# Linear attention and a GELU MLP on one core: k and v nine tokens to a partition, kv in two row tiles, first MLP blocks by token quarters, another load order, stores from ScalarE's queue

## Chip, cores, metric

One Trainium2 chip, one core. The metric is the device time of one launch in microseconds, as the median of several runs. For one core a run's state is taken from its time alone; every run below counts as fast. Each set of runs below was made on one chip with the kernel before beside it, so kernels are compared by their ratio to before. The granted clock is the TensorE clock that the profile shows for a stretch, 1.00 being full speed. PSUM is the memory that matmuls write to, in banks. In the diffs below, comments behind `#` are mine.

## The reference

```python
phi = lambda x: np.where(x > 0, x, np.exp(x) - 1.0) + 1.0        # q, k, v: (8, 8, 576, 64) float32
kv  = einsum('bhsd,bhse->bhde', phi(k), v);  z = phi(k).sum(axis=2)
att = einsum('bhsd,bhde->bhse', phi(q), kv) / (einsum('bhsd,bhd->bhs', phi(q), z)[..., None] + 1e-6)
x   = att.transpose(0, 2, 1, 3).reshape(4608, 512)
out = gelu_tanh(x @ w_in) @ w_out                                # w_in (512, 2048), w_out (2048, 512)
```

## The kernel before

A sequence has 576 tokens: 512 of them ("main") lie four to a partition, and the 64 left over ("rest") of two sequences share one tile. The MLP runs in nine blocks of 512 tokens (eight batches, then all rests together): 16 h steps (w_in, then gelu on ScalarE), then 16 o steps (w_out). Work of other batches is put behind a numbered step of a block (`at(block, step, fn)`), so program order on each engine is set by hand. Cut to what the argument touches:

```python
for c in range(C):                                   # kv of one head pair: 4 matmuls of all 128 rows ...
    nc.tensor.matmul(dst, lhsT=kp[:, c, P*i:P*(i+1)], rhs=vps[b%2][:, 2*i:2*i+2, c, :], start=(c==0), stop=False)
nc.tensor.matmul(dst, lhsT=kr[r, 0, P*i:P*(i+1)], rhs=vrs[..][b%2][r, 2*i:2*i+2, :], start=False, stop=True)  # ... and the rest

for c in range(C + 1):                               # prologue: numerator of batch 0
    if c < C:
        nab_mm(qt[:, c], kvbds[0], n_ps); x_c.append(nab_evac(n_ps))
        keep_warm(2)                                 # matmuls of zeros
    if c >= 1:
        t_x(x_c[c-1], tv); nc.scalar.copy(xt[:, :, P*(c-1):P*c], tv[:, 0:NP, :])
# ... then gelu table, block 0

load_slots = {2: (0, 8), 3: (0, 27), 4: (1, 22)}     # batch 4 is loaded behind step 22 of block 1
# batch 1: exps at (0,15), kv at (0,19), numerator at (0,23..26)
# batch 3: prepare at (1,15): exps 15, phi k 17, cast v 19, phi q 22; numerator of batch 2 at (1,15),(1,17),(1,19),(1,21)
# x and q of batches 2.. are transposed by DMA from SyncE's queue; stores and loads use the same queue
```

## Time and profile before

| | before |
|---|---|
| time, median | 322.5 us |
| span in the profile | 320.0 us |
| third h step of block 0 ends | 26.6 us |
| first o step of block 0 | 37.8 us |
| third h step of block 1 ends | 66.7 us |
| first h step of block 2 | 102.9 us |

The marks cut the span at places that both kernels have. A mark is read from the timeline: the start of the row of h or o matmuls, plus 0.863 us for each step of four matmuls, or 0.83 us for the last 12 short ones where tokens come in quarters.

### The profile page before, as it was taken

The numbers are of one execution on the slowest core, as the hardware profiler recorded it, in microseconds if no ns is written. First come the engines' busy times: TensorE is split into PE (matmuls) and PEld (weight loads), VectorE is DVE, ScalarE is ACT, GpSimd is POOL, SyncE is SP. The second block draws the span as 40 slices with busy tenths as digits, with TensorE's granted clock in tenths as the row PEclk, the third lists the DMA queues.
The fourth block names the chain that finished last, engine by engine and source line by source line (L and its number), as shares of the span: only waits on it lengthen the run. The fifth ranks groups of instructions, "written<-read, shape, count | busy, mean of one in ns | idle before, by whom it ended". The sixth has DMA issues, their size and how long they took to land.

```text
span 320.0 us, 4083 instructions
## 1 busy us (share of the span) xinstructions
PE 294.1 (92%) x1586; PEld 141.6 (44%) x1586; DVE 128.1 (40%) x239; ACT 160.7 (50%) x215; POOL 9.4 (3%) x22
## 2 busy tenths in 40 slices
PE   8969929969969976999999999999999999999993
PEld 3534415524524532445445544544454444444441
DVE  3763077666394223853191439335533000000011
ACT  4737792096723553725744583568355036216500
POOL 6040000000000000000000000000000000000000
PEclk9999978998979997999999999999999999999998
DMA  7999989952115996966599458630245110011022
GB/s 260 340 405 380 387 264 361 359 200 66 34 40 78 283 323 117 338 159 144 117 355 186 132 151 294 198 64 3 66 147 69 66 68 0 0 66 68 0 66 67
DMA packets 75332, 53.74 MB, mean 168 GB/s; under 512 B 44081, under 2 KB 68657, under 8 KB 75313
## 3 DMA queue, kind: packets, MB, share of 16 engines
q1 hardware_dynamic: 75312, 53.49, 56.5%
q8 instruction: 12, 0.20, 0.3%
q14 instruction: 8, 0.06, 0.1%
HBM read 36.70 MB, written 9.44 MB: 144 GB/s over the span
## 4 chain that ended last, share of the span: by engine, by line
PE 68%; DVE 2%; DMA 1%; ACT 1%; issue 0%; DVEq 0%
PE o_ps L557 33%; PE h_ps L538 30%; PE n_ps L236 2%; PE kv_ps L200 1%; DMA xt<-x 1%; DVE k_p L157 1%; ACT k_e L148 1%; DVE x L248 0%; PE kv_ps L208 0%; DVE k_e L153 0%; DVE o_sb L572 0%; DVE o_sb L569 0%; ACT o_sb L570 0%; DVE r L246 0%; DVEq L569 0%
## 5 line engine op out<-in xcount | busy, mean ns | idle before, releaser
L557 PE MATMUL o_ps<-w_out_sb,g 128*128 128x512 bf16 x576 | 130.4, 384 | 0.0
L538 PE MATMUL h_ps<-xt,w_in_sb 128*128 128x512 bf16 x512 | 122.1, 385 | 3.6 <-ACT g L545 2.9
L545 ACT ACTIVATE g<-h_ps 128x512 bf16<-128x512 f32 x144 | 85.4, 597 | 55.9 <-PE h_ps L538 55.8
L557 PEld LDWEIGHTS <-g 128*128 128x128 bf16 x576 | 56.5, 99 | 66.9 <-issue 3.8
L538 PEld LDWEIGHTS <-w_in_sb 128*128 128x128 bf16 x576 | 54.7, 98 | 62.5 <-issue 7.0
L574 ACT COPY o_sb<-o_ps 128x512 f32<-128x512 f32 x17 | 10.0, 585 | 81.0 <-PE o_ps L557 45.6
L572 DVE COPY o_sb<-o_ps 128x512 f32<-128x512 f32 x18 | 12.4, 686 | 64.6 <-PE o_ps L557 64.6
L248 DVE TENSOR_TENSOR x<-n_ps,r 128x512 bf16<-128x512 f32 x36 | 24.9, 691 | 6.5 <-DMA xt<-x 5.3
L225 DVE CAST kvbd<-kv_ps 64x260 bf16<-64x260 f32 x15 | 6.4, 427 | 36.4 <-PE kv_ps L208 36.3
L246 DVE RECIPROCAL r<-n_ps 128x8 f32<-128x8 f32 x36 | 7.4, 206 | 33.7 <-PE n_ps L236 33.7
L153 DVE TENSOR_SCALAR k_e<-k_e 128x2048 bf16<-128x2048 bf16 (+1 forms) x9 | 5.7, 637 | 37.1 <-ACT k_e L148 32.7
L157 DVE SCALAR_TENSOR_TENSOR k_p<-k_x,k_e 128x512 bf16<-128x512 f32 (+1 forms) x36 | 20.3, 626 | 0.3
L157 DVE SCALAR_TENSOR_TENSOR q_p<-q_x,q_e 128x512 bf16<-128x512 f32 (+1 forms) x36 | 20.3, 626 | 0.3
L200 PE MATMUL kv_ps<-vp,k_p 128*128 128x130 bf16 x128 | 13.4, 231 | 6.0 <-DVE vp L185 6.0
L236 PE MATMUL n_ps<-kvbd,qt 128*128 128x130 bf16 x128 | 13.0, 224 | 4.8 <-DVE x L248 4.3
L288 PE MATMUL w_ps<-warm 128*128 128x512 bf16 x50 | 14.8, 445 | 1.2 <-DVE warm L120 1.2
L200 PEld LDWEIGHTS <-k_p 128*128 128x128 bf16 x128 | 10.3, 102 | 12.5 <-issue 4.0
L236 PEld LDWEIGHTS <-qt 128*128 128x128 bf16 x128 | 9.6, 99 | 12.9 <-issue 4.0
L538 PE MATMUL h_ps<-xt_rest,w_in_sb 128*128 128x512 bf16 x64 | 14.0, 379 | 0.0
L148 ACT ACTIVATE k_e<-k_x 128x2048 bf16<-128x2048 f32 x7 | 13.4, 1911 | 0.1
L148 ACT ACTIVATE q_e<-q_x 128x2048 bf16<-128x2048 f32 x7 | 13.3, 1897 | 0.0
L185 DVE CAST vp<-v_x 128x2048 bf16<-128x2048 f32 x7 | 8.5, 1220 | 0.0
(52 smaller groups left out, 105.1 us busy)
## 6 DMA issues: line engine op xcount, KB each, us to landing
out_dram<-o_sb SPq DMA_DIRECT2D x16, 512.0 KB, 3.1
k_x<-in_k_dram SPq DMA_DIRECT2D x7, 1024.0 KB, 6.9
q_x<-in_q_dram SPq DMA_DIRECT2D x7, 1024.0 KB, 9.0
v_x<-in_v_dram SPq DMA_DIRECT2D x7, 1024.0 KB, 9.4
w_st<-in_moe_w_in_dram SPq DMA_DIRECT2D x4, 1024.0 KB, 10.1
w_st<-in_moe_w_out_dram SPq DMA_DIRECT2D x4, 1024.0 KB, 10.7
k_x<-in_k_dram SPq DMA_DIRECT2D x2, 512.0 KB, 4.2
q_x<-in_q_dram SPq DMA_DIRECT2D x2, 512.0 KB, 6.5
```

The costliest lines, as they stand in the source:

```text
L148: nc.scalar.activation(e, ld[name, b], AF.Exp)
L157: nc.vector.scalar_tensor_tensor(xp[:, c, hs, :], xv[:, c, hs, :], 0.0, ev[:, c, hs, :], op0=ALU.max, op1=ALU.add,)
L185: fn(out=vps[b % 2][:, s, :, 0:D], in_=ld["v", b][:, s].rearrange("p h (c d) -> p h c d", d=D),)
L200: nc.tensor.matmul(dst, lhsT=kp[:, c, P * i : P * (i + 1)], rhs=vps[b % 2][:, 2 * i : 2 * i + 2, c, :], start=(c == 0), stop=False,)
L236: nc.tensor.matmul(n_ps[rows, i // 2, 2 * E * (i % 2) : 2 * E * (i % 2) + 2 * E], lhsT=qt_c[:, i, rows], rhs=kvbd[:, i, :], skip_group_che ...
L248: nc.vector.tensor_tensor(x, n_v[:, :, :, 0:D], r[:, :, :, None].to_broadcast([P, 2, 4, D]), op=ALU.mult,)
L288: nc.tensor.matmul(w_ps, lhsT=warm[:, 0:P], rhs=warm)
L538: nc.tensor.matmul(h_ps, lhsT=w_in_sb[:, c, P * m : P * (m + 1)], rhs=xt[:, c, :], start=(c == 0), stop=(c == KM - 1),)
L545: nc.scalar.activation(g[:, m, :], h_ps, AF.Gelu_apprx_tanh)
L557: nc.tensor.matmul(o_ps, lhsT=g[:, m, P * t : P * (t + 1)], rhs=w_out_sb[:, m, :], start=(m == 0), stop=(m == MM - 1),)
L572: nc.vector.tensor_copy(dst, o_ps)
L574: nc.scalar.copy(dst, o_ps)
```

## The change

Its intent: no small loads and no rest matmuls for k and v; the prologue's MLP starts as soon as 128 tokens are ready; weights come before batch 1, whose attention then no longer stands in TensorE's way with its data missing; SyncE no longer holds stores. The diff, cut to its core (`...` marks cuts):

```diff
-    def load_main(src, b, name, eng, parts=1): ...   # 4 tokens a partition, 1024-byte runs
-    def load_rest_half(src, t, m, s, eng): ...       # 64 tokens, 256-byte runs
+    def pairs(src, b):                               # two heads fill 128 partitions, 9 tokens each, 2304-byte runs
+        return src[b].rearrange("h s d -> (h s d)").rearrange("(u n f) -> n u f", n=P, f=J * D)
...
+    def kv_mm(b, ii, kv_ps, js=range(J)):
+        for j in js:                                 # 9 tokens
+            for a in range(2):                       # even heads in rows 0-63, odd heads in rows 64-127
+                r = slice(HP * a, HP * (a + 1))
+                nc.tensor.matmul(kv_ps[:, a, 2*E*ii:2*E*(ii+1)], lhsT=kp[r, j, 2*ii:2*ii+2, :],
+                                 rhs=vp[r, j, 2*ii:2*ii+2, :], start=(j == 0), stop=(j == J - 1), ...)
...
+        nab0(0); nab0(1)                             # prologue: no keep_warm in this loop any more
+        for c in range(C):
+            xs[c] = nab_evac(n_pss[c]); t_x(xs[c], t_ps)
+            if c + 2 < C: nab0(c + 2)
+            nc.scalar.copy(xt[:, :, P*c:P*(c+1)], t_ps)
+            for m in range(QUARTERS):                # QUARTERS = 3: h steps 0..2 on these 128 tokens
+                h_mm(h_pss[m], xt, m, slice(P*c, P*(c+1)))
... # batch 1: cast v, transpose q at (0,30), kv and the same chunk loop at (0,31)
+        at(j, 30, lambda: cast_v(b, slice(0, 1), nc.scalar.copy))
+        at(j, 30, lambda: cast_v(b, slice(1, NP), nc.vector.tensor_copy))
... # block 1: h 0-7, o fourths 0-1, h 8-15, o fourths 2-3
+    plan_prepare(2, 1, 7, (0, 1, 3, 5))
+    plan_attention(2, 1, (16, 17, 18, 19), 19, (21, 23, 25, 27))   # kv in four pieces
+    plan_prepare(3, 1, 23, (0, 1, 4, 5))             # phi of k of batch 3 at step 24
+    at(*((1, 28) if b == 4 else (b - 3, 15)), lambda b=b: load_batch(b))
-            nc.sync.dma_start(out=ov[:, t - 1 : t + 1, :], in_=o_sb)
+            nc.scalar.dma_start(out=ov[:, t - 1 : t + 1, :], in_=o_sb)
```

## The prediction

> **What bounds the kernel now.** I read the page first (busy shares), then the table of stretches, then the timeline around each place where TensorE's clock or busy share drops, and last the chain that ended last.
>
> ```profile
> PE 294.1 (92%) x1586; PEld 141.6 (44%) x1586; DVE 128.1 (40%) x239; ACT 160.7 (50%) x215; POOL 9.4 (3%) x22
> 24.02 13.97 PE L538 MATMUL h_ps<-xt,w_in_sb 128*128 128x512 bf16 x64 [0.67 <-ACT xt L345]
> 186.20 13.81 PE o_ps L557 x64
> 171.54 0.23 PE kv_ps L200 x4
> ```
>
> TensorE is the bound. In the chain a run of 64 MLP matmuls takes 13.81 us, 215.8 ns each, and there are 18 such runs (9 token blocks, two layers): 18 x 13.81 = 248.6 us that the change leaves alone. The other 71 us of the 320.0 us span are: the prologue until the first MLP matmul (24.0), the tail after the last (4.8), attention matmuls between the MLP ones, and waits. From 140 to 260 us there are no waits at all: one block takes 29.7 us there (140.10 to 169.82), 27.6 of MLP plus 1.16 for kv (four groups of five matmuls, 0.29 each) plus 0.93 for the numerator (4 x 0.23). So the waits sit in the first 128 us:
>
> ```profile
> 47.46 0.59 PE L200 MATMUL kv_ps<-vp,k_p 128*128 128x130 bf16 x4 [6.02 <-DVE vp L185]
> 71.48 5.30 PE L538 MATMUL h_ps<-xt,w_in_sb 128*128 128x512 bf16 x16 [2.91 <-ACT g L545]
> 92.68 0.59 PE L236 MATMUL n_ps<-kvbd,qt 128*128 128x130 bf16 x4 [2.82 <-DVE x L248]
> 122.81 0.66 PE L236 MATMUL n_ps<-kvbd,qtr 128*64 128x130 bf16 x8 [4.69 <-DVE x L248]
> ```
>
> The bracket is TensorE's idle time before the row and what ended it: 6.02 + 2.91 + 2.82 + 4.69 = 16.4 us. Each costs more than itself. The table of stretches (us from:to, length, busy time of PE, PEld, DVE, ACT, POOL with counts, granted clock, DMA share, GB/s) shows the clock behind each:
>
> ```profile
> 47.46:51.50 4.04, 4.04 (x26) 2.86 (x26) 3.96 (x8) 2.36 (x2) 0.00 (x0) 0.55 1.08 381
> 71.50:75.10 3.60, 3.60 (x9) 1.29 (x9) 3.50 (x7) 2.49 (x6) 0.00 (x0) 0.53 0.02 5
> 92.70:95.60 2.90, 2.90 (x11) 1.28 (x12) 2.83 (x5) 0.00 (x0) 0.00 (x0) 0.52 0.22 45
> 122.80:127.00 4.20, 4.19 (x25) 1.76 (x26) 0.90 (x2) 1.66 (x2) 0.00 (x0) 0.59 0.60 64
> ```
>
> Lost: 4.04 x 0.45 + 3.60 x 0.47 + 2.90 x 0.48 + 4.20 x 0.41 = 6.6 us more. The waits are worth about 23 us, and that is what a change of order can win.
>
> **What the Trainium skill says.** "TensorE: Matmul & The Clock Gate", Part 1, says that the array falls to half clock after an idle window of about 3.4 us and needs about as long to recover. The trace agrees on the recovery (0.52 to 0.59 for 2.9 to 4.2 us), but idle times of 2.8 and 2.9 us were already enough here. "TensorEngine Tiling (Array Packing)", Key Properties, says that different tiles work in parallel but that changing the tiling mode drains the array. The trace has both:
>
> ```profile
> 15.00 0.23 PE L208 MATMUL kv_ps<-vr,kr_p 64*128 64x130 bf16 x1
> 15.16 0.41 PE L200 MATMUL kv_ps<-vp,k_p 128*128 128x130 bf16 x4
> 184.79 0.44 PE L236 MATMUL n_ps<-kvbd,qtr 128*64 128x130 bf16 x8
> 185.16 1.04 PE L538 MATMUL h_ps<-xt,w_in_sb 128*128 128x512 bf16 x4
> ```
>
> In the prologue one 64-row matmul stands between groups of four full ones, and the period is 0.50 us (15.00 to 15.50) where the all-128-row groups later take 0.29: 0.21 us for a switch there and back. The eight half-column matmuls at 184.79 take 0.37 us with the switches in it, where 8 x 0.058 = 0.46 would be serial: the halves overlap in part. "DMA: Bandwidth & Descriptors", Issuing engines are not separate DMA queues, says a second issuing queue saves only the issuing sequencer's time; so moving stores to ScalarE frees SyncE's order, not bandwidth. "ScalarE activation tables: per-element evaluation and per-set limits", What a function is on this engine, gives 1283 ns for a table load; the trace has 1283.
>
> **The change part by part.**
>
> Prologue, to the end of the third h block (before: 24.02 + 3 x 0.863 = 26.6 us). Loads: the first 2.2 MB (q and k halves) had landed by 9.7 us before and will again, then v by about 12.8. ScalarE: the last exp of k 9.5 to 10.7 (1.06 x 1152/1024 = 1.17), the table load, now early, to 12.0, the qt copy (1.0) to 13.0, casts of v to 14.8. VectorE's phi of 1024 + 1152 elements twice ends near 13.2. So kv starts at 14.2 and ends at 15.4; its two evacuations end at 16.45 (before 17.16), x0 is ready at 17.85 (before 18.58). From there the old loop took 1.43 us a chunk and then began MLP. The new one does 12 matmuls of 128 columns per chunk as soon as the chunk is copied: transposes 0.4, copy 0.65, 12 x 0.058 = 0.7, in order on TensorE, 1.76 us a chunk. First quarter at 19.0, the last ends at 19.0 + 3 x 1.76 + 0.7 = 25.0. **Gain 1.6.**
>
> From there to the third h block of block 1 (before 66.7, so 40.1 us). Thirteen h blocks end at 36.2. k of batch 1 (after 10.75 MB, at 360 to 390 GB/s about 34.5 us) and q (37) now arrive before ScalarE is free. ScalarE: table, exps (2 x 1.17, 2 x 1.06), table, until 44.0. VectorE: two phi_k of 2.0 and phi_q of 3.45 end near 47. v lands at 43. So kv of batch 1 is put at the end of the o run (50.9), and the 6.02 us wait and its cold clock (1.8) go. But now nothing lies beside that attention: transposes 0.95, kv 1.2, qt copies and evacuations to about 53.7, x0 at 55.1, then four chunks of 1.76 with the quarters in them, ending at 62.2. 62.2 - 25.0 = 37.2. **Gain 2.9.**
>
> Block 1 to its end (before 66.7 to 103.1, 36.4 us). New order: 8 h, two fourths of o, 8 h, the rest. The exps of batch 2 lie beside o, so the 2.91 wait on gelu and its 1.7 of cold clock go. New waits: kv of batch 2 is at slot 16, nine steps (7.8 us) after the exps; ScalarE and VectorE need about 9.5 (gelu end 0.8 after, table 1.28, exp 2.15, clamp 0.77, four of 0.76, cast 1.37): 1.7 us. And the 2.82 wait comes back larger. The exps of batch 3 are at slot 23, phi_k at 24, and the evacuations of the numerator of slots 25 and 27 stand behind phi_k in VectorE's order. From the last h to x: 0.8 + 1.28 + 2.15 + 0.77 + 3.05 + 0.95 = 9.0 us; TensorE has 4 x 0.863 + 0.5 = 3.95 us of work until it needs that buffer. Wait 5.1, then 1.7 of cold clock. Sum: 25.0 of MLP + 1.8 kv + 0.9 + 1.7 + 5.1 + 1.7 = 36.2. **Gain 0.2.**
>
> Blocks 2 to 8 and the tail (before 216.9). The wait of 4.69 was a chain: x buffers stood full because their transposes queued on SyncE behind loads of 64-row rests (3.5 us of issue each) and behind stores. The rests of k and v are gone, and the stores are on ScalarE; it and its cold clock (1.7) go. kv now has 36 matmuls of 64 rows in four pieces. At the pace of the column halves (0.37/8 = 0.046 with switches) that is 1.66; at 18 pairs of 0.058 plus 4 x 0.21 it is 1.88. I take 1.8, so 0.64 more than 1.16, five times: 3.2. 193.4 MLP + 5 x 2.73 + 1.5 for the query rests + 4.8 tail = 213.4. **Gain 3.5.** VectorE and ScalarE get somewhat longer k and v pieces (2304 for 2048) but keep slack in every block.
>
> Span 25.0 + 37.2 + 36.2 + 213.4 = 311.8; the time is 2.5 us above the span (322.5 against 320.0): **314.3 us**, 2.5% less.
>
> **Rivals.** (1) *The row tiles do not overlap.* Then kv costs 36 x 0.058 + 0.84 = 2.9 us a batch, 6 us more over the remaining batches: 321, the same. For it: only the column form is in this trace; and two weight loads per pair may not fit in 0.058. Against: the overlap of the halves. (2) *The wait in block 1 is not there or hidden*, because the chain ScalarE, VectorE is shorter than I add up: 307 to 309. For it: the author tuned these slots. Against: the same chain produced the 2.82 wait, and it now has two steps less to hide in. (3) *The attention of batch 1, alone on TensorE, drops the clock* or store issue on ScalarE delays its copies (load traffic is heaviest there; one store issue took 1.92 us at its longest): 316 to 319. (4) *The front gains more*, since k and v come in runs of 2304 bytes, not 1024: prologue 1 us shorter, 313.
>
> **Range and chances.** The terms I am least sure of are kv (-1 to +6), the wait in block 1 (-6 to +2) and batch 1's attention (-1 to +4). That makes 307 to 321. The 2% line is 316.1, close to the middle: faster 0.60, within 2% 0.36, slower 0.04.
>
> **What would show it.** h block 3 starts near 25; no 6 us wait for vp near 47; iteration 1 has h rows with no wait on g at its start, but an n_ps row near 88 us waiting about 5 us for DVE x, with a clock near 0.5 behind it; no n_ps wait on xt transposes near 115; later blocks 30.3 us and kv pieces of 0.4 to 0.5 us. The prediction is wrong if that wait is missing, or if a later block takes over 31 us.

## The result, and the profile after

325.9 us against 322.5: 1.013 times before (95% interval 1.009 to 1.016). Ratios here are the mean time of one kernel's fast runs over that of the other's of the same rounds, so not quite the ratio of the medians quoted. The prediction of 314.3 us with 321 as its upper end was wrong; the change is slightly slower. Measured once more in a later set of runs (after_again), it was 1.012.

| mark (us) | before | predicted | after | after_again |
|---|---|---|---|---|
| third h step of block 0 ends | 26.6 | 25.0 | 24.5 | 27.2 |
| first o step of block 0 | 37.8 | 36.2 | 38.7 | 39.6 |
| third h step of block 1 ends | 66.7 | 62.2 | 67.0 | 66.1 |
| first h step of block 2 | 102.9 | 98.4 | 102.6 | 102.6 |
| span | 320.0 | 311.8 | 323.9 | 322.4 |

The table of marks says where to look. In the first profile the prediction loses 3.0 us between the first two marks, 2.3 in the next stretch, gains 0.6 in block 1 and loses 7.9 from block 2 on: 311.8 - 0.5 + 3.0 + 2.3 - 0.6 + 7.9 = 323.9. In the second profile of the same kernel (after_again, whose rows are read like the others) the four stretches up to block 2 lose 2.2, 1.2, 0.5 and 0.4 us instead: other places, and about the same sum. TensorE's waits of over 1.1 us behind the prologue's start of work, in the timeline of the changed kernel (first profile):

```profile
13.81 1.25 PE L225 MATMUL kv_ps<-vp,k_p 64*128 64x130 bf16 x36 [1.56 <-ACT vp L215]
25.77 0.43 PE L275 MATMUL h_ps<-xt,w_in_sb 128*128 128x512 bf16 x1 [1.22 <-ACT g L285]
80.31 0.46 PE L225 MATMUL kv_ps<-vp,k_p 64*128 64x130 bf16 x10 [1.22 <-DVE vp L215]
97.18 0.40 PE L246 MATMUL n_ps<-kvbd,qt 128*128 128x130 bf16 x4 [4.73 <-DVE x L258]
122.83 0.65 PE L246 MATMUL n_ps<-kvbd,qtr 128*64 128x130 bf16 x8 [4.36 <-DVE x L258]
```

The waits of 6.02 and 2.91 us are gone, as predicted. The one near 97 is the predicted 5.1. The one at 122.8 was to go and is there, nearly as long as before (4.36 us for 4.69). The second, 1.22 us, is new. I read it so: the first whole h step takes over PSUM banks from the prologue's three h tiles and waits until the gelus have read them (a_pool tests this). And the clock falls where no long wait stands (table of stretches, same columns as in the prediction; the changed kernel first, then the kernel before):

```profile
16.00:20.00 4.00, 2.55 (x36) 2.12 (x36) 2.65 (x7) 2.00 (x3) 1.90 (x1) 1.00 1.06 389
24.00:28.00 4.00, 2.56 (x15) 1.29 (x14) 0.00 (x0) 2.01 (x4) 2.75 (x2) 0.75 1.06 388
28.00:32.00 4.00, 4.00 (x17) 1.65 (x16) 0.00 (x0) 1.99 (x5) 2.94 (x2) 0.83 1.05 388
56.00:60.00 4.00, 2.11 (x18) 1.68 (x18) 1.74 (x5) 0.96 (x2) 0.00 (x0) 0.59 1.05 393
60.00:64.00 4.00, 3.76 (x37) 3.48 (x36) 1.12 (x3) 0.78 (x2) 0.00 (x0) 0.56 1.05 324
```

```profile
16.00:20.00 4.00, 2.66 (x21) 1.29 (x19) 2.20 (x5) 0.63 (x2) 3.20 (x2) 1.00 1.05 408
24.00:28.00 4.00, 3.98 (x19) 1.85 (x19) 1.91 (x3) 3.39 (x5) 0.00 (x0) 1.00 1.07 394
28.00:32.00 4.00, 4.00 (x20) 1.76 (x18) 0.56 (x1) 2.67 (x6) 0.00 (x0) 1.00 1.11 364
56.00:60.00 4.00, 3.84 (x33) 2.27 (x33) 3.08 (x9) 0.00 (x0) 0.00 (x0) 1.00 1.11 332
60.00:64.00 4.00, 4.00 (x26) 2.07 (x25) 2.48 (x5) 0.58 (x1) 0.00 (x0) 1.00 1.09 386
```

Before, the clock was 1.00 in all of them. In this profile the changed kernel runs at 0.75 and 0.83 where its first whole h steps stand, and at little over half clock in the first two of batch 1's four chunks (12 matmuls of 128 tokens take 1.44 us there and 0.83 in the other two).

What stands in SyncE's queue ahead of the transposes that the wait at 122.8 is for (SyncE's timeline, changed kernel; the second column is the time the issue takes):

```profile
108.31 0.58 SPq L80 DMA_DIRECT2D k_x<-in_k_dram  x1
108.95 1.09 SPq L90 DMA_DIRECT2D q_x<-in_q_dram  x2
110.15 1.08 SPq L80 DMA_DIRECT2D v_x<-in_v_dram  x1
111.74 3.25 SPq L470 DMA_TRANSPOSE qtr<-qr_p  x1
115.11 8.79 SPq L460 DMA_TRANSPOSE xt<-x  x4
```

And two lines of the same queue in the kernel before, where rests do stand in front, as the prediction read:

```profile
105.58 3.49 SPq L75 DMA_DIRECT2D v_r<-in_v_dram  x2
117.49 6.39 SPq L435 DMA_TRANSPOSE xt<-x  x4
```

Stores and k and v rests are gone from the changed kernel's queue, and yet its four transposes take 8.8 us to issue. The first three lines are the loads of batch 4: 1.18 + 1.05 + 1.18 = 3.4 MB. They are issued at 108.3, 5.5 us later than the first of batch 4's loads before (102.8).

### The profile page after: what moved, and what is told of

It reads as the page before. It is cut to its first block, busy times and chain, and to the rows that moved or that the text cites. A ratio compares the mean times of both kernels' runs of the same rounds, so it can differ in the third digit from the quotient of the medians.

```text
span 323.9 us, 4353 instructions
## 1 busy us (share of the span) xinstructions
PE 293.5 (91%) x1732; PEld 141.0 (44%) x1763; DVE 118.6 (37%) x210; ACT 165.2 (51%) x222; POOL 16.4 (5%) x20
## 4 chain that ended last, share of the span: by engine, by line
PE 80%; DVE 4%; ACT 3%; DMA 2%; issue 1%; ACTq 0%; DVEq 0%
PE h_ps L275 38%; PE o_ps L600 36%; PE kv_ps L225 3%; PE n_ps L246 2%; DMA xt<-x 2%; DVE k_p L175 2%; ACT k_e L178 1%; DVE vp L215 1%; ACT L178 1%; ACT xt L536 1%; DVE x L258 1%; PE t_ps L268 0%; DVE k_e L172 0%; DVE o_sb L559 0%; ACT g L285 0%
## 5 line engine op out<-in xcount | busy, mean ns | idle before, releaser
L600 PE MATMUL o_ps<-w_out_sb,g 128*128 128x512 bf16 x564 | 128.9, 386 | 0.9 <-issue 0.2
L275 PE MATMUL h_ps<-xt,w_in_sb 128*128 128x512 bf16 (+1 forms) x567 | 123.7, 361 | 5.9 <-ACT xt L378 2.2
L275 PEld LDWEIGHTS <-w_in_sb 128*128 128x128 bf16 x648 | 58.4, 100 | 63.9 <-issue 9.1
L172 DVE TENSOR_SCALAR k_e<-k_e 128x2304 bf16<-128x2304 bf16 (+1 forms) x10 | 6.6, 656 | 53.4 <-ACT k_e L178 53.4
L175 DVE SCALAR_TENSOR_TENSOR k_p<-k_x,k_e 128x576 bf16<-128x576 f32 x32 | 22.3, 754 | 0.3
L178 ACT ACTIVATE k_e<-k_x 128x2304 bf16<-128x2304 f32 (+1 forms) x10 | 17.3, 1738 | 1.0 <-DMA k_x<-in_k_dram 0.9
L178 ACT ACTIVATE q_e<-q_x 128x2048 bf16<-128x2048 f32 (+1 forms) x10 | 15.5, 1556 | 3.0 <-DMA q_x<-in_q_dram 3.0
L225 PE MATMUL kv_ps<-vp,k_p 64*128 64x130 bf16 x288 | 12.8, 218 | 4.0 <-DVE vp L215 2.1
L225 PEld LDWEIGHTS <-k_p 64*128 64x128 bf16 x288 | 8.3, 94 | 14.8 <-issue 10.9
L215 DVE CAST vp<-v_x 128x2304 bf16<-128x2304 f32 (+2 forms) x8 | 10.8, 1353 | 0.0
```

The costliest lines, as they stand in the source:

```text
L175: nc.vector.scalar_tensor_tensor(o, x, 0.0, e, op0=ALU.max, op1=ALU.add)
L178: nc.scalar.activation(e[:, s], ld[name, b][:, s], AF.Exp)
L215: fn(out=vps[b % 2][:, :, us, 0:D].rearrange("p j u d -> p u j d"), in_=ld["v", b][:, us].rearrange("p u (j d) -> p u j d", d=D),)
L225: nc.tensor.matmul(kv_ps[:, a, 2 * E * ii : 2 * E * (ii + 1)], lhsT=kp[r, j, 2 * ii : 2 * ii + 2, :], rhs=vp[r, j, 2 * ii : 2 * ii + 2, :] ...
L275: nc.tensor.matmul(h_ps[:, ts], lhsT=w_in_sb[:, c, P * m : P * (m + 1)], rhs=xt[:, c, ts], start=(c == 0), stop=(c == KM - 1), skip_group_ ...
L600: nc.tensor.matmul(o_pss[t], lhsT=g[:, m, P * t : P * (t + 1)], rhs=w_out_sb[:, m, :], start=(m == 0), stop=(m == MM - 1),)
```

## The experiments

Theory after the result, in four parts. **L**: the wait in block 2 comes from batch 4's loads in front of the x transposes, not from stores and rests. **C**: the two stretches with little work for TensorE lose the clock, and that ate what the prologue and batch 1 should have gained. **H**: the hand-over of PSUM banks costs 1.2 us. **K**: kv costs more in pieces because TensorE changes between whole and half rows. Rivals: the stores and rests (my prediction's step), too few x buffers, a clock that doesn't matter because TensorE waits for others anyway, row halves that don't overlap.

### Batch 4's loads earlier, in both kernels

```diff
-        at(*((1, 28) if b == 4 else (b - 3, 15)), lambda b=b: load_batch(b))      # a_load4
+        at(*((1, 13) if b == 4 else (b - 3, 15)), lambda b=b: load_batch(b))
```
```diff
-        at(*load_slots.get(b, (b - 3, 15)), lambda b=b: load_batch(b))      # b_load4; for batch 4 this was step 22 of block 1
+        if b == 4:
+            at(1, 8, lambda: load_batch(4, "kqv"))       # with the rests of k and v
+            at(1, 22, lambda: load_batch(4, "r"))        # the rest of q alone
```

> The changed kernel with one edit: the loads of batch 4 are issued at step 13 of block 1 instead of step 28. Theory L (loads in front): in block 2 of both kernels the transposes of x stand in SyncE's queue behind batch 4's loads (3.4 MB, some 9 us of traffic), so x's buffers stay full and TensorE waits 4.4 us near 122.8 us with half a clock for 5.6 us after it. Then the wait near 122.8 goes, and the time falls from 325.9 by about 6.5 us to 319 to 320. Rival S, the step of my prediction: the wait comes of stores and small rest loads in SyncE's order; both are already gone in the changed kernel, so moving these loads would change nothing (within 1 us). Rival X: three x buffers are too few whatever the queue does; the wait then stays too.

> The kernel before, with batch 4's loads (k, q, v and the rests of k and v) issued at step 8 of block 1 instead of step 22; the rest of q stays at 22, for its buffer comes free late. Theory L: TensorE's wait of 4.69 us near 122.8 and its cold clock go here too: 322.5 falls to about 316.5. Rival S (stores and the small rests are what holds the transposes up): the rest loads of q and the stores still stand in front, so 1 to 3 us at most.

Measured: a_load4 321.2 us, 0.997 of before (0.992 to 1.003), so 1.5% below the changed kernel's 1.012; b_load4 316.4 us, 0.982 (0.976 to 0.988). In block 2 the matmuls for the query rest follow without a bracket in both. In a_load4:

```profile
105.35 1.89 PE L275 MATMUL h_ps<-xt,w_in_sb 128*128 128x512 bf16 x8 [1.45 <-DMA xt<-x]
121.20 0.43 PE L246 MATMUL n_ps<-kvbd,qtr 128*64 128x130 bf16 x8
```

The wait is gone in both kernels, so L holds, and the wait was there without the change. A caution: b_load4 moves the rests of k and v along with the loads, so what these rests cost in the kernel before is not separated; a_load4 has no such rests, so there it is the loads alone. The query rest's transpose takes 3.25 us to issue behind the loads (above) and 1.19 us in a_load4. In a_load4 the loads now stand in front of batch 2's transposes and cost 1.45 us there: its gain is 5 us and not the 6.5 expected. X falls, and for the changed kernel S falls.

### Stores from ScalarE's queue alone

```diff
-            nc.sync.dma_start(out=ov[:, t - 1 : t + 1, :], in_=o_sb)      # the kernel before, both stores
+            nc.scalar.dma_start(out=ov[:, t - 1 : t + 1, :], in_=o_sb)
```

> The kernel before with one edit: its stores are issued from ScalarE's queue. The step of my prediction: stores in SyncE's order are part of what held the transposes of x up in block 2; then the wait of 4.69 us near 122.8 shrinks by 1 to 3 us and the time by 1 to 4. Theory L (batch 4's loads in front): the wait stays at 4 us or more and the time within 1 us of before.

Measured: 322.2 us, 1.000 of before (0.995 to 1.006). The wait is even longer in its profile:

```profile
122.20 0.66 PE L236 MATMUL n_ps<-kvbd,qtr 128*64 128x130 bf16 x8 [5.45 <-DVE x L248]
```

Moving the stores is worth nothing in time, which is the second half of why my step failed.

### PSUM pools, then matmuls of zeros

a_pool opens the main pools (six banks "ho", one pair "a") at the start and uses them in the prologue. a_poolwarm adds zeros:

```diff
-        keep_warm(2)                      # before kv of batch 0
+        keep_warm(7)                      # also 2 more before the numerator, 4 after it, 2 in each chunk
...
+            kv_evac(b, kv_ps, ...); warm1(5)          # batch 1; 5 after the numerator, 2 in each chunk
```

> The changed kernel with the PSUM pools of the main part used from the start, in place of three prologue pools that are given back (numerator single-buffered in the prologue, as in batch 1). Theory H (hand-over): the h block after the first three waits 1.2 us for the three gelus because its banks are taken over from the prologue's; that wait goes and the time falls by about 1 us. The clock of the prologue is not helped by it: a stretch of 3 to 8 us near half clock between 12 and 32 us, as in the four runs of the changed kernel so far. Rival: the single-buffered numerator costs what the hand-over gives: 0.

> As a_pool, with TensorE fed with matmuls of zeros in its gaps: 5 more before kv, 2 more before the numerator, 4 after it, 2 in each chunk of batch 0; 5 after kv, 5 after the numerator and 2 in each chunk of batch 1. Theory C (clock): in the changed kernel TensorE is so lightly used in these two stretches that the granted clock falls to about half (0.50 to 0.75 in 56 to 64 us, and a stretch in 12 to 32 us), which the kernel before avoided with such matmuls. Then the clock is 1.00 in both stretches and the time is 3 to 5 us below a_pool. Rival: TensorE waits for ScalarE and VectorE there, so the clock doesn't matter: within 1 us of a_pool, or slower by the fed matmuls.

Measured: a_pool 324.3 us, 1.006 (1.000 to 1.012); a_poolwarm 320.6 us, 0.995 (0.990 to 0.999). The 1.22 us hand-over is gone in both. In a_pool the clock stayed low (0.74 over 12 to 32 us); in a_poolwarm it is 1.00 (table of stretches, a_poolwarm):

```profile
16.00:20.00 4.00, 3.81 (x40) 2.41 (x39) 1.80 (x4) 2.00 (x4) 2.08 (x2) 1.00 1.07 391
24.00:28.00 4.00, 4.00 (x28) 2.14 (x27) 0.00 (x0) 3.26 (x6) 2.46 (x3) 1.00 1.05 387
56.00:60.00 4.00, 3.92 (x51) 2.91 (x49) 2.31 (x6) 1.39 (x3) 0.00 (x0) 1.00 1.05 369
60.00:64.00 4.00, 3.76 (x37) 2.36 (x35) 0.25 (x1) 2.65 (x5) 0.00 (x0) 1.00 1.10 302
```

Its marks: first o step at 35.8 us (predicted 36.2), third h step of block 1 at 62.3 (61.45 for the last quarter, plus 0.83; predicted 62.2). With the clock held and the banks not handed over, the prologue and batch 1 together take what the prediction worked out for them; two small misses cancel, the first o step 0.4 us early and batch 1 0.5 us long (26.5 for 26.0). C holds; the clock is the term that was missing there. (In batch 1 the kernel before had kept the clock with o steps between the chunks, not with zeros.) The clock over 12 to 32 us in the profiles of the eight kernels that lack the zeros before kv (the changed kernel in two, a_load4, a_kphi, a_onepiece, a_pool, a_cast, a_noq) was 0.91, 0.74, 0.74, 0.83, 0.91, 0.74, 0.91, 0.91; in the four of the old kernel and in the four with enough zeros (a_poolwarm, a_pw_load4, a_all, a_all2) it was 1.00 each time. The first five of the eight run the same instructions there, so place and length of the loss change from one execution to the next: 20 us x 0.09 to 0.26, 1.8 to 5.2 us of clock. From 56 to 64 us it is the same: 0.57 to 0.62 in the first profile, a_load4, a_kphi and a_onepiece, and 1.00 in after_again, with equal instructions.

### The token quarters undone

```diff
-    QUARTERS = 3
+    QUARTERS = 0           # and keep_warm(2) in each chunk of the prologue
```

> The changed kernel without the token quarters (first three h blocks of blocks 0 and 1 as whole blocks), with two matmuls of zeros per chunk in the prologue as the kernel before had. What the quarters are worth by themselves: in the prologue the chunk loop took 1.73 us a chunk with them (TensorE in order: transposes, copy, 12 matmuls), and would take about 1.0 without, so four chunks and three h blocks end at about the same time (24.6) and nothing is lost. Theory C adds that the zeros keep the clock up in the prologue, so it would be some 1 to 2 us faster there; batch 1's chunks have no zeros and stay cold. Expected -1 to -2 us. If the quarters do what they are meant for, it is 2 to 4 us slower.

Measured: 326.0 us, 1.012 (1.006 to 1.018), the same as the changed kernel. Block 0's first o step came at 36.4 us, 2.3 earlier than in the first profile of the changed kernel, for the clock was 1.00 from 20 us on and no banks were handed over; batch 1's chunks, without quarters and without zeros, gave it back (third h step of block 1 at 67.8 us, five whole steps before the o steps at 72.15: 31.4 us behind the first o step, for 28.3). So in the prologue the quarters give about nothing in the form they have: in order on TensorE, transposes, a copy to wait for and 12 short matmuls make a chunk 1.73 us, and from the first numerator to the end of the third h step it is 8.5 us with them and 8.25 without. In batch 1 it is 3.1 us longer without them, but at a clock of 0.50 to 0.52 from 60 to 68 us; what they are worth there is not separated, the less so as the edit adds zeros too. I had expected 1 to 2 us less, so that was a miss.

### v's cast, whole and early

```diff
-        at(j, 30, lambda: cast_v(b, slice(0, 1), nc.scalar.copy))
-        at(j, 30, lambda: cast_v(b, slice(1, NP), nc.vector.tensor_copy))
+        at(j, 27, lambda: cast_v(b, slice(0, NP), nc.vector.tensor_copy))
```

> The changed kernel with batch 1's cast of v as one VectorE instruction of four head pairs at step 27 of block 0, in place of one pair on ScalarE and three on VectorE at step 30. The three-pair form took 1.95 us for 1728 elements where four pairs take 1.36 for 2304, and it stood behind o's copy. Expected: the cast takes 1.36 us and ends before 51 us, the kv matmuls of batch 1 start about 1.0 us earlier (53.4 for 54.4), and the time falls by about 1 us. Rival: the qt copies on ScalarE are what comes last; then 0 to 0.3.

Measured: 323.1 us, 1.003 (0.998 to 1.008), about 3 us under the changed kernel instead of 1. The groups by form in the changed kernel (busy us, mean ns):

```profile
L215 DVE CAST vp<-v_x 128x2304 bf16<-128x2304 f32 x6 | 8.1, 1355 | 0.0
L215 DVE CAST vp<-v_x 128x1728 bf16<-128x1728 f32 x1 | 1.9, 1947 | 0.0
L215 DVE CAST vp<-v_x 128x576 bf16<-128x576 f32 x1 | 0.7, 749 | 0.0
```

Three pairs cost 1.13 ns an element and one 1.30, four cost 0.59: the odd numbers of pairs here run at about half the rate. In a_cast the cast took 1.36 us, and kv of batch 1 began at 53.0 for 54.4. Of these 1.4 us, 0.4 were there at the first o step (38.2 for 38.7), so the cast gave 1.0, as expected. The rest of the gain I put down to the clock, which was 1.00 and not 0.56 from 60 to 64 us in its profile; that changes from one execution to the next, so only 1.0 us of the 3 is shown.

### phi of k of batch 3 later

```diff
-    plan_prepare(3, 1, 23, (0, 1, 4, 5))
+    plan_prepare(3, 1, 23, (0, 4, 4, 5))
```

> The changed kernel with one edit: phi of k of batch 3 at step 27 of block 1, behind the last numerator's evacuation in VectorE's order, instead of step 24. The predicted step: TensorE's wait of 4.73 us near 97 us is the evacuation standing behind phi_k; it goes, with its cold clock (about 1.6 us): 325.9 to 319.5 to 321. Rival: VectorE's work is only moved, and TensorE waits instead at the start of block 2 (for o's banks or for vp): a fall of under 2 us.

Measured: 323.8 us, 1.006 (0.999 to 1.012), 0.7% under the changed kernel, 2 us of the 5 to 6. The 4.73 us wait is gone, and these are in its place:

```profile
99.53 0.46 PE L225 MATMUL kv_ps<-vp,k_p 64*128 64x130 bf16 x10 [0.32 <-DVE vp L215]
104.79 2.08 PE L275 MATMUL h_ps<-xt,w_in_sb 128*128 128x512 bf16 x8 [0.84 <-DVE o_sb L559]
121.29 0.66 PE L246 MATMUL n_ps<-kvbd,qtr 128*64 128x130 bf16 x8 [6.57 <-DVE x L258]
```

Block 2 begins 5.2 us earlier (97.3), but the wait on the x transposes grows from 4.36 to 6.57 and two small ones come up. The cause of the wait was right; as long as the loads stand in front, most of the repair is handed back.

### kv in one piece

```diff
-            ii, part = n // 2, n % 2
-            kv_mm(b, ii, box["kv"], range(0, 5) if part == 0 else range(5, J))
+            if n == 3: kv_mm(b, 0, box["kv"]); kv_mm(b, 1, box["kv"])
```

> The changed kernel with one edit: the kv matmuls of batches 2 to 7 stand at one step instead of in four pieces, so TensorE changes from whole to half rows and back once per batch, not four times. If the extra cost of kv (1.87 us a batch beside the 1.16 of before) is mostly the switches (0.21 us for a pair), six batches save 6 x 3 x 0.2 = 3.6 us: 322 to 323. If it is the matmuls (no overlap of the halves), under 0.7 us is saved. Pieces of 0.39 and 0.33 us in the trace, and 36 matmuls in 1.22 us for batch 1, speak for the first.

Measured: 319.6 us, 0.993 (0.987 to 0.999), 2.0% (6 us) under the changed kernel. First the chain of the changed kernel in a later block, then the timeline of a_onepiece:

```profile
175.98 0.39 PE kv_ps L225 x10
176.37 0.97 PE h_ps L275 x4
177.34 0.33 PE kv_ps L225 x8
```

```profile
105.62 1.20 PE L225 MATMUL kv_ps<-vp,k_p 64*128 64x130 bf16 x36
106.75 1.90 PE L275 MATMUL h_ps<-xt,w_in_sb 128*128 128x512 bf16 x8
```

In pieces, a kv piece and the h step after it take 0.39 + 0.97 = 1.36 and 0.33 + 0.97 = 1.30 us; the h step alone is 0.863. Two of each make 5.32 - 3.45 = 1.87 us of kv a batch. In one piece, kv takes from the end of the h run (101.21 + 20 x 0.2158 = 105.53) to 106.75: 1.22 us. So the switches are what kv paid for, 0.65 us a batch, and the halves do overlap (36 x 0.058 would be 2.1). K holds and rival 1 of the prediction falls. That is 3.9 us for six batches; the wait of 1.22 us at 80.3 goes too, as kv of batch 2 now comes three steps later. The remaining microsecond or so is not separated from the clock's chance.

### Together

a_pw_load4 is a_poolwarm with a_load4's edit: only what the prediction had missed most, the clock and the loads.

> a_poolwarm and a_load4 together. If my prediction failed only by the clock in the two light stretches and by the wait in block 2, and its other terms hold, repairing these two must bring the kernel to the predicted size: a_poolwarm's span of 318.4, less the 3.6 us of wait and about 0.6 of clock behind it, plus up to 1.5 for the wait of the transposes of batch 2 behind the moved loads: span 313 to 315, time 315 to 317 (predicted 314.3), ratio to before 0.980 to 0.985. Rival: one repair gives the other's gain back, and the time stays at 319 or above.

Measured: 315.7 us, 0.979 (0.976 to 0.981), span 313.4. The two repairs add up, and the kernel lands 1.4 us above the predicted 314.3; its one new wait, 1.30 us for batch 2's transposes, is about that.

a_all has every repair, with k and q of batch 4 loaded at step 0 of block 1, v at step 13, and phi of q of batch 3 at step 30:

> All repairs: one set of PSUM pools with matmuls of zeros, v cast early and whole, kv in one piece, batch 4's k and q loaded at the start of block 1 and its v at step 13, phi of k of batch 3 behind the last numerator and phi of its q behind the evacuation of o. From a_poolwarm's 318.4 of span: wait in block 2 -4.2, wait in block 1 with its clock (none now) -5 to -6, kv in one piece -4 to -5, cast -1: 303 to 305, time 305 to 307.5, ratio 0.945 to 0.955. If the waits only move (as in a_kphi), 309 to 312.

Measured: 307.5 us, 0.953 (0.950 to 0.957). One wait of over 0.5 us is left behind the start:

```profile
92.04 6.99 PE L277 MATMUL h_ps<-xt,w_in_sb 128*128 128x512 bf16 x20 [3.77 <-DMA xt<-x]
```

a_all2 moves v of batch 4 and the second query rest's loads to step 29, behind batch 2's transposes.

```diff
-    at(1, 13, lambda: load_batch(4, "v"))
+    at(1, 29, lambda: load_batch(4, "v"))         # and load_q_rest(1) from step 14 to 29
```

> a_all with the loads of v of batch 4 and of the second query rest issued at step 29 of block 1, behind the transposes of batch 2's x, in place of steps 13 and 14. Theory L: the 3.77 us wait of block 2's first h near 92 us goes, and up to 2 us of it comes back as a wait for batch 3's q transposes, which now stand behind these loads: 307.5 falls to 303.5 to 305.5, ratio 0.941 to 0.947. If the transposes are slow by themselves, it stays at 307.

Measured: 304.3 us, 0.948 (0.942 to 0.953), correct, and the fastest of all. The wait is gone and comes back as 1.64 us for the q transposes, the expected amount; the clock is 1.00 on average:

```profile
98.38 0.41 PE L248 MATMUL n_ps<-kvbd,qt 128*128 128x130 bf16 x4 [1.64 <-DMA qt<-q_p]
```

b_best repairs the two order faults of the kernel before: b_load4, with phi of k, cast of v and phi of q of batch 3 at steps 21, 22 and 23 of block 1.

```diff
-            plan_prepare(b, b - 2, 15)
+            plan_prepare(b, b - 2, 15, (6, 7, 8) if b == 3 else (2, 4, 7))
```

> b_load4 with phi of k of batch 3 behind the last numerator of block 1 as well (steps 21, 22, 23 for 17, 19, 22): the 2.82 us wait near 93 us and its 1.4 us of clock go, if they aren't given back at the start of block 2. From b_load4's ratio of 0.982: 0.968 to 0.975, 312.5 to 314.5 us. The change's parts are then worth the distance to a_all2, some 8 to 10 us; if b_best is at 306 or below, they are worth next to nothing and only order counted.

Measured: 312.8 us, 0.972 (0.968 to 0.977). Its two remaining waits are those that the change removes, 6.02 and 2.91 us. a_all2 is 2.5% below it (0.948 over 0.972), so the change is worth having once its own losses are mended. How much of that is the new order of batch 1 and block 1, which removes the two waits, and how much its other parts is not separated.

after_again is the changed kernel unedited:

> The changed kernel once more, unedited, on the chip of these runs, as the yardstick: 1.008 to 1.016 of before by every theory, and a stretch of clock under 0.9 somewhere in 12 to 32 us, at a place that need not be that of the first profile.

Measured: 326.1 us, 1.012 (1.008 to 1.017). As expected, the clock loss in the prologue was there, and at another place than in the first profile: 0.63, 0.50 and 0.59 in the four-microsecond stretches from 12 to 24 us, and 1.00 from 24 to 32. Batch 1 tells more, for here it kept the clock without any zeros (1.00 from 56 to 64 us):

```profile
56.00:60.00 4.00, 1.58 (x32) 1.20 (x27) 1.65 (x5) 0.96 (x2) 0.00 (x0) 1.00 1.06 396
```

The stretch from the first o step to the third h step of block 1 then took 26.5 us: as long as with zeros (26.5), near the predicted 26.0, and 1.9 us less than in the first profile (28.3). That is theory C once more, with not one instruction changed. It also means that the two stretches do not lose the clock in every execution.

## Why the prediction was wrong

- **The prologue, "Gain 1.6".** The third h step ended at 24.5 for 25.0, but with luck: the clock fell just behind it, and in after_again, where it fell earlier, the step ended at 27.2. The step that failed is the assumption that the h steps after it run at full pace: the hand-over of banks (1.2 us) was not seen, and the clock was lost (1.7 us in the first profile, behind the mark). a_pool and a_poolwarm show both.
- **Batch 1, "Gain 2.9".** The rival "batch 1, alone on TensorE, drops the clock" was named, but put at 316 to 319 us and left in the tail of the range. It happened in the first profile: 0.59 and 0.56 from 56 to 64 us, 1.9 us of time; in after_again it did not, and there the prologue lost more. With zeros, the mark is at 62.3 for the predicted 62.2. A second term was missing from the sum: v's cast, whose three pairs took 1.95 us on VectorE; kv waited 0.89 us for it, and a_cast shows 1.0.
- **Block 1, "Gain 0.2".** Right in kind and size: wait 4.73 for 5.1, 1.22 for 1.7, the stretch 35.6 for 36.2 us.
- **Blocks 2 to 8, "it and its cold clock go".** This is the largest error, 7 us of the 8 there: 4.36 us of wait and 5.6 us at half clock. The step said that rests and stores in SyncE's order held the transposes up, so that the wait would go with them. The stores do not matter (b_store), and the changed kernel, with neither in the queue, still waits; a_load4 shows that there the 3.4 MB of batch 4 in front are the cause. The change moved these loads from step 22 to step 28. Whether the rests of k and v had a share in the kernel before, which the later loads took back, stays open: no run has the changed kernel with the loads at step 22.
- **kv, 1.8 us a batch.** Measured 1.87, and a_onepiece shows that the mechanism (halves overlap, switches cost) was right.
- **Stores.** The prediction counted them in; they are worth nothing (b_store, 1.000).

The clock term and the loads term are the whole miss to within 1.5 us: a_pw_load4 mends just these (and the bank hand-over) and stands at 315.7 us, inside the predicted range. The gain existed, but most of it was lost again at once to the lower clock, and the wait that was to go in block 2 never had the cause that I gave it.

What stays open: which measure of TensorE's activity sets the clock. The kernel before had a busy time of 2.66 us of 4 from 16 to 20 us and kept 1.00; the changed kernel had 2.55 there and lost it later, and after_again kept 1.00 with 1.58 of 4 from 56 to 60. And about 2 us of a_cast's and 1 us of a_onepiece's gain are not separated from that chance.

## What to carry to other kernels

When work is taken from a stretch where TensorE had been kept busy on purpose, count what is left for it there, at half clock, before counting the gain; fed matmuls of zeros cost nothing here, where TensorE waits anyway (batch 1 took 26.5 us with them, and 26.5 without them at full clock). For a wait on a DMA transpose, read the queue's own timeline and ask what bytes stand in front, before blaming the number of issues. And take two waits that follow each other as one: repairing the first alone hands its gain to the second.

## What the Trainium skill lacked or had wrong

- "TensorE: Matmul & The Clock Gate", Part 1, ties the fall to half clock to an idle window of about 3.4 us; here an idle time of 2.8 us was enough (kernel before, 89.9 to 92.7 us). Its section "A second HAM failure mode: psum-queue depth-cycling" says that short idles between groups of matmuls also make the clock swing, and the runs here agree: it fell in stretches of short matmuls without any wait over 1.6 us (0.50 to 0.83 in stretches between 12 and 32 us, 0.56 to 0.59 from 56 to 64 in one of its two profiles). What it lacks is how much idleness that takes, and, beyond the ramp at a kernel's start, how far it varies: the same instructions lost 1.8 us in one profile and 5.2 in another.
- "TensorEngine Tiling (Array Packing)", Key Properties, says that a mode change drains the array but gives no size. Here kv in four pieces instead of one cost 0.65 us a batch, three more switches there and back: 0.22 us for one.
- "VectorE: DVE Perf Modes", What auto-detection actually checks, asks that the outermost dimensions of source and destination be even or equal. A float32 to bfloat16 cast of three pairs (both sides written as 3 x 9 x 64) took 1.95 us for 1728 elements, about half the rate of four pairs, which took 1.36 for 2304. That fits the rule if the source, which is contiguous, counts as one dimension; the page does not say so, and no run here shows it.
- "DMA: Bandwidth & Descriptors" has no figure for a DMA transpose that stands behind loads in one queue: here one transpose took 3.25 us to issue behind 3.4 MB, and 1.19 us where the loads had gone ahead (a_load4).
- No page has that PSUM tiles of a new pool wait for the readers of the old pool's banks: 1.22 us here.
